# Seven-product matrix multiplication with K split into 256 + 256 + 64 or into 288 + 288: the last rows in one matmul per product

## The chip, the cores and the metric

One core of one Trainium2 chip. The metric is the device time of one execution, in microseconds (us); three executions of the kernel before were timed, and one more was profiled.

## The reference

x is 2048 x 576. It is normalised row by row, and three things are summed: x itself, a sliding attention (32 heads of 18, a window of 8 keys at distances 0, 2, ..., 14), and a dense block with ReLU.

```python
xn = (x - mean) / sqrt(var + 1e-5)
q, k, v = split(xn @ wqkv)                 # 576 x 1728, 32 heads of 18
o = softmax(q . k[s - 2w] * 18**-0.5) @ v[s - 2w]      # w = 0..7, masked before the start
h = maximum(xn @ w1, 0)                    # 576 x 4608
return x + o @ wo + h @ w2                 # wo 576 x 576, w2 4608 x 576
```

All inputs and the output are float32.

## The kernel before, in words

**Precision.** TensorE multiplies in a shortened float32 form (fp32r). Each operand is cut into a high part (ScalarE copies it, which rounds) and a low part (VectorE subtracts: `hi_lo`), and a product is the sum of three terms: high by high, high by low, low by high.

**Two halves of x.** x is worked through in two halves (`ph` 0 and 1) of 1024 rows; a half lies transposed in SBUF, in `h` = 0, 1 and `j` = 0, 1, groups of 256 columns. The first products are `xn @ w1` (18 sets of 256 features per half, kind F) and `xn @ wqkv` (7 sets, kind Q): 25 sets per half, 50 in all, each with two steps `t` (one per `h`).

**Seven products for eight.** From t = 4 on (sets 2 to 49) a step takes K = 576 as 256 + 256 + 64. The first 512 rows and the 256 features of a set are a 2 by 2 block matrix, multiplied by Strassen's scheme in Winograd's form: seven products P1 to P7 (`pstep`) of sums of weight blocks (made by VectorE in `set_make`: c1 to c4) by sums of x blocks (`s_forms`). Each is six matmuls (three terms by two groups of 128 rows; `terms`). The last 64 rows, `RR`, are not in the scheme: four of the products (P5, P2, P3, P4) take two more matmuls for them (`rest`), with x's high and low parts stacked in 128 rows (`XR`). Sets 0 and 1 are multiplied without the scheme (`classic`, 14 matmuls per product) in the opening.

**Results.** F results go through ReLU and a high/low split into one of six buffers `HB` (`h_parts`), and output steps `o_step` multiply them by `w2` into PSUM (`po`), six matmuls each. Q results are turned and stored in DRAM (`qd`), and attention is done by VectorE from there: `fetch` loads K, V and Q of one of four units, `attention` forms products with the window, softmax and the weighted sum; its output is turned through DRAM and multiplied by `wo` along with later output steps.

**Weights.** `w1`, `wqkv` and `w2` are copied in the first half to packed DRAM buffers (`w1c`, `wqc`, `w2c`) by DMAs on POOL's queue (`kept_part`, paced by a small POOL copy that follows ScalarE's `hb`). `set_make(s)` is called one set ahead, in step t = 2s - 2: four loads of 128 KB and two of 64 KB (the last 64 rows twice, for high and low), then the sums, then high and low parts into `wset`, of which there are two.

**Order.** The program is written out by a planner, `Order`. PE's order is fixed by the loops and, up to t = 4, by the list `OPEN`: B and O are output steps, T turns a tile of x, Q and F are products of sets 1 and 0, K copies a set to its packed buffers, S makes sums of x, M makes set 2. ScalarE's and VectorE's operations are put between by estimated durations, when their inputs are ready, by due times. Attention waits in a list `back`, which VectorE takes from when nothing else is ready soon. SP issues most DMAs in the planner's order, and an issue waits there for what it depends on; each engine works strictly in the order written.

**The second half of x** is loaded, normalised and turned during t = 47 to 51 (`x_load`, `x_norm`, `x_raw`, `x_rest`, `x_parts`, `x_done`), after the last attention unit of the first half.

Of the kernel before, what the change touches and what calls it, by code (L numbers as in the profile page):

```python
# [16 lines left out]
P = 128  # L17
NPH = 2
NI = 8
# [10 lines left out]
NHB = 6  # L30
# [10 lines left out]
T1, B11, T2, B21, T3, B22, T4, RR = range(8)  # L41
B12 = T3

PE, ACT, DVE, SP, PL = "pe", "act", "dve", "sp", "pool"
TAIL = {PE: 0.24, ACT: 0.13, DVE: 0.13}
# [3 lines left out]
class Op:  # L49


    __slots__ = ("eng", "dur", "fn", "after", "due", "end", "lag", "then", "post", "gate")

    def __init__(self, eng, dur, fn, after, due, lag=0.0):
        self.eng, self.dur, self.fn, self.due, self.lag = eng, dur, fn, due, lag
        self.after = [a for a in after if a is not None]
        self.end = None
        self.then = None
        self.post = None
        self.gate = None  # L60


class Order:
# [4 lines left out]
    def __init__(self):  # L68
        self.clk = {PE: 0.0, ACT: 0.0, DVE: 0.0, SP: 0.0, PL: 0.0}
        self.dma = 0.0  # L70
        self.gp = 0.0
        self.wait = {ACT: [], DVE: []}
        self.back = deque()
# [14 lines left out]
    def give(self, op, start):  # L88
        op.fn()
        self.clk[op.eng] = start + op.dur  # L90
        op.end = start + op.dur + TAIL[op.eng] + op.lag
        if op.then:
            op.then.end = self.gp = max(self.gp, op.end) + op.then.dur
        if op.post:
            op.post()

    def pick(self, eng):
        now = self.clk[eng]
        best, soon = None, None
        for op in self.wait[eng]:  # L100
            r = self.ready(op)
            if r is None:
                continue
# [7 lines left out]
        if eng == DVE and self.back:  # L111
            op = self.back[0]
            r = self.ready(op)
            if r is not None:
                s = max(now, r)
                if soon is None or s + op.dur <= soon[1] + self.SLACK:
                    return op, s
        return soon

    def step(self, limit):  # L120
        best = None
        for eng in (ACT, DVE):
            c = self.pick(eng)
            if c and c[1] < limit and (best is None or c[1] < best[1]):
                best = c
# [9 lines left out]

    def hurry(self, op, due):
# [5 lines left out]
    def force(self, ops):  # L142
        for op in ops:
            if op is None:
                continue
            self.hurry(op, -1.0)
            while op.end is None:
                if op in self.back:
                    assert self.step(FAR)
                else:  # L150
                    assert self.step(FAR), "an operation waits for what is not given out"
# [10 lines left out]

    def later(self, fn, n, after=(), lag=0.0):
# [4 lines left out]
    def send(self, fn, kb, after=(), margin=0.0):  # L168

        after = [a for a in after if a is not None]  # L170
        self.force(after)
# [9 lines left out]
    def keep(self, fn, kb, after=0.0):  # L181

        fn()
        op = Op(PL, 1.0, None, (), 0.0)
        self.clk[PL] = max(self.clk[PL], self.now(), after) + kb / 90.0
        op.end = self.clk[PL] + 3.0
# [21 lines left out]
def tile_body(ctx: ExitStack, tc: tile.TileContext, x, wqkv, wo, w1, w2, out):  # L208
# [6 lines left out]
    DR = D - KT * P  # L215
    D2 = D // 2
# [54 lines left out]
    mvp = pool("mvp", 6)  # L271
# [5 lines left out]
    act, dve, send, pe = o_.act, o_.dve, o_.send, o_.pe  # L277

# [9 lines left out]
    XR = [keep.tile([P, 3, TBN], F32R, name=f"xr{h}") for h in range(2)]  # L288
    keep.tile([P, PADS[0]], F32, name="pad0")
    BUF = [keep.tile([P, 2, 2048], F32R, name=f"wset{b}") for b in range(2)]  # L290
    keep.tile([P, PADS[3]], F32, name="pad4")
    HB = [keep.tile([P, 2, TBN], F32R, name=f"hb{b}") for b in range(NHB)]
    WHB = [keep.tile([P, 2, TBN], F32R, name=f"oh{b}") for b in range(2)]
    keep.tile([P, PADS[3]], F32, name="pad5")
# [15 lines left out]
    def wset(s):  # L310
        return BUF[s % 2].rearrange("p e (s k c) -> p e s k c", s=8, k=2)
# [27 lines left out]

    def mm(o, l, r, start, stop):  # L340
        nc.tensor.matmul(o, l, r, start=start, stop=stop, skip_group_check=True)  # L341

    def hi_lo(hi, lo, raw, n, after, slack, behind=(), by_pool=False):

        if by_pool:
            def both():
                copy(hi, raw)
                nc.gpsimd.tensor_tensor(lo, raw, f32(hi), op=ALU.subtract)

            a = act(both, n, after, slack)  # L350
            a.then = b = Op(PL, 0.0055 * n, None, (), 0.0)
            return [a, b]
# [9 lines left out]
    TURNED = [0] * NI  # L362
# [6 lines left out]
    def normalise(i, src, after, slack, by_act=False, alloc=True):  # L369
# [8 lines left out]
        def rest():  # L378
            z["mv"] = mv = mvp.tile([P, 2], F32, name="mv")
            z["r"] = r = mvp.tile([P, 1], F32, name="rstd")  # L380
# [3 lines left out]
            if by_act:  # L384
                z["nm"] = nm = mvp.tile([P, 1], F32, name="nm")
# [14 lines left out]

        if by_act:
            MEANS[i] = b
            NORMED[i] = act(one, D + 200, [b], slack + 1.0)
        else:
            NORMED[i] = dve(two, D // 2 + 100, [b], slack + 1.0)

    def turn_pe(i, pa, pb, after=()):
        def f():
            if pa is not None:
                for k in range(KT):  # L410
                    nc.tensor.transpose(pa[:, k * P : (k + 1) * P], XN[i][:, TURNED[i] + k * P : TURNED[i] + (k + 1) * P], ident)
            if pb is not None:
                nc.tensor.transpose(pb[0:DR, 0:P], XN[i][:, KT * P : D], ident)

        return pe(f, 0.11 * ((KT if pa is not None else 0) + (pb is not None)), [NORMED[i], *after])
# [7 lines left out]
    def xt_direct(i, pa, pb, t, slack, free):  # L423
# [7 lines left out]
        r1 = act(lambda: copy(XR[h][0:DR, j, c], pb[0:DR, 0:P]), 128, [t], slack + 1)  # L431
        r2 = dve(lambda: sub(XR[h][DR:P, j, c], pb[0:DR, 0:P], f32(XR[h][0:DR, j, c])), 128, [r1], slack + 1.5)
        if j == 0:
            r3 = act(lambda: copy(RD[h][0:DR, c], pb[0:DR, 0:P]), 128, [t, *free], slack + 4)
        else:
            r3 = dve(lambda: sub(RD[h][0:DR, c], RD[h][0:DR, c], pb[0:DR, 0:P]), 128, [t, *RAWR[h]], slack + 2)
        XOK.setdefault((h, j), []).extend([k1, k2, r1, r2])
        XHL.append((k1, k2))
        RAW.setdefault((h, j), []).append(k3)
        RAWR.setdefault(h, []).append(r3)  # L440
        return [k1, k2, k3, r1, r2, r3]
# [3 lines left out]
    def s_forms(h, slack):  # L445
# [15 lines left out]
        r = act(lambda: copy(XR[h][0:DR, 2], RD[h][0:DR]), TBN, RAWR[h], slack + 3)  # L461
        ok.append([r, dve(lambda: sub(XR[h][DR:P, 2], RD[h][0:DR], f32(XR[h][0:DR, 2])), TBN, [r], slack + 3.5)])
        XOK[h, 10 + S1], XOK[h, 10 + S2], XOK[h, 10 + S4] = ok
        return [z for y in ok for z in y]

# [46 lines left out]

    def set_make(s, fine=False):
# [6 lines left out]
        w = wset(s)  # L520
        z = f32(w)[:, 1]
        got = {}
        free = slots_free(s % 2, range(8))

        def rest_rows():
            for rows in slice(0, DR), slice(DR, P):
                got[RR] = send(
                    lambda rows=rows: nc.sync.dma_start(z[rows, RR, :, 0:wd], src_[KT * P : D, :].rearrange("r (k c) -> r k c", k=2)),
                    64, [*there, *free], late,
                )  # L530

        for rows, f, b in ((0, 0, B11), (0, 1, B12), (256, 1, B22), (256, 0, B21)):
            ts = b == B12
# [1042 lines left out]
```

## Time and profile before

| | |
|---|---|
| median of three runs | 1112.38 us (1112.16 to 1112.78) |
| the profiled execution, its own time | 1115.05 us |
| its span, first to last instruction | 1113.3 us |
| granted TensorE clock | 0.999 |
| PE busy | 1102.5 us, 9047 matmuls |
| VectorE (DVE) busy | 909.0 us, 1749 instructions |
| ScalarE (ACT) busy | 756.2 us, 1561 instructions |
| GpSimd (POOL) busy | 218.3 us, 434 instructions |
| DMA | 144.15 MB, mean 129 GB/s |

A row of a timeline has start, duration, engine, line, operation, output and inputs, partitions x elements, count, and in brackets the idle time of the engine before it with what ended it. A grouped row has, behind the bar, the busy sum in us, the mean of one in ns, and the idle time before the group by releaser. PEld is the weight load, which runs beside the matmuls; SPq is the queue of SP. Matmul ends are modelled, starts are not. A row of DMA issues has count, KB each and the median us from issue to landing.

### The profile page before, as it was taken

What the parts mean: (1) busy time and instruction counts of PE and PEld (TensorE: products, weight loads), DVE (VectorE), ACT (ScalarE), POOL (GpSimd) and SP (SyncE); (2) the same over time, 40 slices, a digit from 0 to 9 for tenths busy, and PEclk for the clock granted to TensorE, in tenths of its full rate; (3) what the DMA queues carried; (4) which work ended last, traced back from release to release, by engine and by line L of the source; (5) the groups of instructions that cost most, each with busy time, mean ns of one, the idle gap of its engine ahead of it and who ended that gap; (6) DMA issues with size and microseconds to landing.
All of it is one profiled execution on the core that took longest, in us unless ns stands there. A gap on an engine that the chain in (4) does not pass through costs nothing.

```text
span 1113.3 us, 24046 instructions
## 1 busy us (share of the span) xinstructions
PE 1102.5 (99%) x9047; PEld 1098.6 (99%) x9047; DVE 909.0 (82%) x1749; ACT 756.2 (68%) x1561; POOL 218.3 (20%) x434
## 2 busy tenths in 40 slices
PE   9999999999999999999999999999999999999998
PEld 8998999999999999999999999999999999999998
DVE  7867999999999889955885689989998998997440
ACT  6754666566687677676794565656667766766774
POOL 4132384342554423700210000000000000000000
PEclk9999999999999999999999999999999999999999
DMA  7488488856854552463354745563625415224212
GB/s 218 105 187 199 122 216 192 184 145 169 213 158 127 163 151 84 107 158 92 110 173 93 192 93 110 122 137 83 158 76 117 107 52 141 70 56 86 78 49 86
DMA packets 329862, 144.15 MB, mean 129 GB/s; under 512 B 212097, under 2 KB 310401, under 8 KB 328513
## 3 DMA queue, kind: packets, MB, share of 16 engines
q1 hardware_dynamic: 320176, 115.76, 42.3%
q0 software_dynamic: 9408, 26.55, 8.3%
q8 instruction: 71, 1.16, 0.4%
q14 instruction: 47, 0.38, 0.1%
q10 hardware_dynamic: 160, 0.30, 0.1%
HBM read 118.42 MB, written 50.66 MB: 152 GB/s over the span
## 4 chain that ended last, share of the span: by engine, by line
PE 89%; DVE 3%; SPq 3%; DMA 2%; ACT 2%; issue 1%; POOL 0%; DVEq 0%; ACTq 0%
PE po L341 43%; PE bk L341 26%; PE pm L341 12%; PE bkA L341 7%; SPq L1061 1%; DMA qo<-qd 1%; DMA wset<-w1c 1%; DMA qo<-in_w 0%; DVE pr L1107 0%; DMA wqc<-in_wqkv 0%; DVE sn L338 0%; DVE stg L656 0%; DVE wset L338 0%; ACT x L335 0%; ACT hb L335 0%
## 5 line engine op out<-in xcount | busy, mean ns | idle before, releaser
L341 PE MATMUL po<-w2t,hb 128*128 128x256 f32 (+1 forms) x3456 | 503.5, 292 | 0.1
L341 PEld LDWEIGHTS po<-w2t,hb 128*128 128x128 f32 x3456 | 463.2, 187 | 0.4 <-DVE hb L628 0.4
L335 ACT ACTIVATE x<-po 128x576 f32<-128x576 f32 x286 | 186.3, 651 | 231.5 <-PE po L341 230.6
L341 PE MATMUL bk<-xs,wset 128*128 128x256 f32 (+1 forms) x1584 | 224.0, 277 | 0.6 <-ACT sn L335 0.6
L341 PEld LDWEIGHTS bk<-xs,wset 128*128 128x128 f32 (+1 forms) x1584 | 202.3, 187 | 0.9 <-ACT sn L335 0.8
L335 ACT ACTIVATE po<-x 128x576 f32<-128x576 f32 x286 | 187.0, 654 | 6.0
L481 POOL COPY spare<-hb 1x1 f32<-1x1 f32 x192 | 94.6, 493 | 222.8 <-ACT hb L335 222.8
L341 PE MATMUL bk<-xa,wset 128*128 128x256 f32 (+1 forms) x888 | 125.5, 278 | 1.8 <-DVE sn L338 0.9
L341 PEld LDWEIGHTS bk<-xa,wset 128*128 128x128 f32 (+1 forms) x888 | 113.7, 187 | 2.8 <-DVE sn L338 1.1
L341 PE MATMUL pm<-xs,wset 128*128 128x256 f32 (+1 forms) x720 | 102.2, 277 | 0.3 <-ACT bkA L335 0.3
L338 DVE TENSOR_TENSOR sn<-bk,sn 128x256 f32<-128x256 f32 (+1 forms) x132 | 55.2, 419 | 52.3 <-ACT hb L335 25.3
L341 PEld LDWEIGHTS pm<-xs,wset 128*128 128x128 f32 (+1 forms) x720 | 92.0, 187 | 0.7 <-ACT bkA L335 0.5
L1107 DVE TENSOR_TENSOR pr<-qo,kk 128x1152 f32<-128x1152 f32 x64 | 85.4, 1346 | 7.9 <-DMA qo<-qd 6.9
L1113 POOL TENSOR_SCALAR_AFFINE_SELECT lg<-lg 1x512 f32<-1x512 f32 x8 | 9.6, 1206 | 415.1 <-DVE lg L1110 415.1
L341 PE MATMUL bkA<-xa,wset 128*128 128x256 f32 (+1 forms) x624 | 88.3, 278 | 0.5 <-ACT bkA L335 0.5
L1110 DVE TENSOR_REDUCE lg<-pr 128x64 f32<-128x1152 f32 x64 | 85.3, 1340 | 0.2
L1139 DVE TENSOR_TENSOR pr<-lg,v 128x1152 f32<-128x1152 f32 x64 | 85.2, 1348 | 0.2
L341 PEld LDWEIGHTS bkA<-xa,wset 128*128 128x128 f32 (+1 forms) x624 | 81.4, 187 | 1.0 <-ACT bkA L335 0.7
L335 ACT ACTIVATE hb<-sn 128x256 fp32r<-128x256 f32 x140 | 57.4, 414 | 35.1 <-DVE sn L338 34.6
L341 PE MATMUL bk<-xr,wset 128*128 128x256 f32 (+1 forms) x412 | 80.4, 276 | 0.0
L338 DVE TENSOR_TENSOR wset<-ts,wset 128x512 fp32r<-128x512 f32 (+2 forms) x98 | 65.1, 665 | 10.5 <-ACT wset L335 10.3
L1146 DVE TENSOR_TENSOR pr<-pr 128x288 f32<-128x288 f32 (+1 forms) x128 | 71.4, 597 | 0.0
(156 smaller groups left out, 1551.8 us busy)
## 6 DMA issues: line engine op xcount, KB each, us to landing
w2t<-w2c SPq DMA_DIRECT2D x70, 288.0 KB, 3.3
qd<-stg SPq DMA_DIRECT2D x216, 64.0 KB, 2.0
wset<-w1c SPq DMA_DIRECT2D x105, 128.0 KB, 2.8
w1c<-in_w POOLq DMA_DIRECT2D x68, 144.0 KB, 3.4
w2c<-in_w POOLq DMA_DIRECT2D x68, 144.0 KB, 3.5
out<-x SPq DMA_DIRECT2D x16, 288.0 KB, 2.2
ts<-w1c SPq DMA_DIRECT2D x35, 128.0 KB, 2.7
wset<-w1c SPq DMA_DIRECT2D x70, 64.0 KB, 2.3
```

What stands on the lines that cost most here:

```text
L335: nc.scalar.activation(o, i, func)
L338: nc.vector.tensor_tensor(o, a, b, op=op)
L341: nc.tensor.matmul(o, l, r, start=start, stop=stop, skip_group_check=True)
L481: nc.gpsimd.tensor_copy(spare[0:1], f32(LATEST[-1])[0:1, 0:1])
L1061: z = send(lambda: nc.sync.dma_start(o, i.rearrange("i p c -> p i c")), cnt * 2, after)
L1107: nc.vector.tensor_tensor(pr[i], q, window(k, i), op=ALU.mult)
L1110: nc.vector.tensor_reduce(s["lg"][:, i], pr.pop(i).rearrange(heads, d=Dh), axis=AX.X, op=ALU.add)
L1113: nc.gpsimd.affine_select(out=z, in_=z, pattern=[[1, NI], [1, W], [0, HG]], compare_op=ALU.is_ge, fill=-1e9 / scale, base=1 - W, channel_m ...
L1139: nc.vector.tensor_tensor(pr[i].rearrange(heads, d=Dh), e, window(VV[u % 2], i).rearrange(heads, d=Dh), op=ALU.mult)
L1146: nc.vector.tensor_tensor(o, z[:, 0:n], z[:, n : 2 * n], op=ALU.add)
```

## The change

K is split into two halves of 288 rows, each 256 + 32 (`ROWS = (0, 288)`). The 32 rows of each half go through the seven-product scheme too. Their three terms lie in one matmul of 128 rows: the weight side holds low, high, high, zero, the x side four copies of the 32 rows of which the first two are high and the last two low. So each product is `terms` and one `rest` matmul:

```diff
+        def go(o, b, xs, xr, start, more):
+            def f():
+                terms(o, slot(m, b), xs, start)
+                rest(o, m, b, xr)
+            return pe(f, T7, [*ok[b], *more])
...
-    def rest(bank, s, f, xr):
-        w, wd = wset(s), wide(s)
-        for e in range(2):
-            mm(bank[0:wd], w[:, e, RR, f, 0:wd], xr, False, e == 1)
+    def rest(o, s, b, xr, stop=False):
+        wd = wide(s)
+        mm(o[0:wd], wset(s)[0][:, b, 2, 0:wd], xr, False, stop)
```

The weights' sums and parts for these rows are made once for four sets at a time, in 128 rows (32 of each set), and kept in DRAM as low, high, high. There are seven batches for the 25 sets; `KK`, the buffer of attention's keys, is the work space. Batches 0 and 1 stand in `OPEN` as W0 and W1; 2 and 3 follow the first attention unit's key products, 4 and 5 the second's, 6 the fourth's, and the next unit's keys are fetched after them.

```diff
+    def batch(b, work, highs, free, slack):
...
+        def there(got):
+            c1 = dve(lambda: sub(raw[0:n, 0:3:2], raw[0:n, 2:5:2], raw[0:n, 1:3]), 2 * P, got, slack)
+            c2 = dve(lambda: sub(raw[0:n, T2], raw[0:n, B22], raw[0:n, T1]), P, [c1], slack + 0.2)
+            c4 = dve(lambda: sub(raw[0:n, T4], raw[0:n, B21], raw[0:n, T2]), P, [c2], slack + 0.4)
...
+                e = [send(lambda: nc.sync.dma_start(RWD[b][0], work[0:n, 0 : 7 * P]), 115 * n // DH, ds)]
...
+                        e.append(send(lambda: nc.sync.dma_start(to[:, y], c), 58 * n // DH, ks))
```

`set_make` loads a set's remainder ready made, in one DMA of 96 rows, in place of the two of 64 rows, and every product of the set waits for it. One part of 512 columns becomes one of 256, because `RR` is gone.

```diff
-                    lambda rows=rows: nc.sync.dma_start(z[rows, RR, :, 0:wd], src_[KT * P : D, :].rearrange("r (k c) -> r k c", k=2)),
-                    64, [*there, *free], late,
+        last = send(
+            lambda: nc.sync.dma_start(
+                f32(hi)[0:R3, :, 2], RWD[b][:, i * DH : (i + 1) * DH].rearrange("a r (s c) -> a r s c", s=7)
+            ), 344, [BDONE[b], *free], late,
+        )
+        ok = {q: [last] for q in range(7)}
```

For sets 0 and 1 in the opening the 32 rows are loaded three times over by a source with a leading repeat:

```diff
+    def thrice(src, r0):
+        return src[r0 : r0 + DH][None].to_broadcast([3, DH, src.shape[1]])
```

The x side: POOL makes the four copies (`fours`, in the tile of the attention's logits), and two transposes per tile turn them; four sums and two pairs of parts per half `h` follow (`s_forms`, `s_rest`, the latter in the place of an `XA` block that only `classic` reads).

```diff
+        def fours():
+            src = XN[i].rearrange("p (q c) -> p q c", q=2)[:, :, 2 * P : 2 * P + DH]
+            nc.gpsimd.tensor_copy(XF[0][:, i % 2], src[:, :, None, :].to_broadcast([P, 2, 4, DH]))
...
+            for q in range(2):
+                z = XF[0][:, i % 2, q].rearrange("p a c -> p (a c)")
+                nc.tensor.transpose(pb[:, q * P : (q + 1) * P], z, ident)
```

To make room in SBUF the hidden buffers fall from six to four. The list `OPEN` is new, in another order, with R (turn a remainder of x) and W (a batch) as added kinds:

```diff
-NHB = 6
+NHB = 4
-B0 T2 B1 T3 Q000 K2 F010 F011 T4 Q011 O0101 T5 O0100 S0 O0110 T6
-Q001 K3 O0111 Q010 T7 F100 F101 F110 O1000 S1 O1001 O1010 F111 M2 K4 O1011
-Q111 Q100 Q110 O1100 O1101 O1111 Q101 O1110
+K2 T2 B0 T3 R2 W0 B1 K3 R3 T4 R4 Q001 F011 S0 T5 Q010 F010 Q000 Q011 T6 R5
+R6 K4 O0100 O0101 O0110 T7 R7 O0111 F100 F111 F101 W1 F110 S1 M2 O1000 Q111
+O1010 O1001 O1011 Q101 Q110 O1101 O1100 O1111 O1110 Q100
```

Further: the planner now also places POOL's operations, and when something is forced it gives out only what that needs; eight transposes of the attention output by VectorE become one instruction; the second half's tiles are loaded in one DMA each instead of two, from t = 47 on in other places; the last group of the first half's attention output is planned one step later.

More of the change, by code (lines that the diff above doesn't have):

```diff
@@ L134, in step, with needs @@
         return True
+    def needs(self, op, out):
+        if op.end is None and op not in out:
+            out.add(op)
+            for a in op.after:
+                self.needs(a, out)
+        return out
     def hurry(self, op, due):
@@ L161, in dve, with gp @@
         return op
+    def gp(self, fn, n, after, slack):
+        op = Op(GP_, 0.0022 * n + 0.2, fn, after, self.now() + slack)
+        self.wait[GP_].append(op)
+        return op
     def later(self, fn, n, after=(), lag=0.0):
@@ L345, in hi_lo @@
         if by_pool:
[L346 to L352, printed above, removed]
+            a = act(lambda: copy(hi, raw), n, after, slack)
+            return [a, o_.gp(lambda: less(lo, raw, f32(hi)), n, [a], slack + 0.8)]
         a = act(lambda: copy(hi, raw), n, after, slack)
```

618 lines of the change are left out of this document (391 added, 227 removed).

## The prediction

> **What bounds the kernel now.** I read the page's busy times and slices first, then busy time by stage, the waits of PE, and the PE timeline. The page:
>
> ```profile
> span 1113.3 us, 24046 instructions
> PE 1102.5 (99%) x9047; PEld 1098.6 (99%) x9047; DVE 909.0 (82%) x1749; ACT 756.2 (68%) x1561; POOL 218.3 (20%) x434
> PE   9999999999999999999999999999999999999998
> PE 89%; DVE 3%; SPq 3%; DMA 2%; ACT 2%; issue 1%; POOL 0%; DVEq 0%; ACTq 0%
> ```
>
> PE is idle for 1113.3 - 1102.5 = 10.8 us in all, and the chain that ended last is PE for 89%. So a matmul taken out should take its time out of the span, unless a new wait is put in its place. Where waits can arise shows by stage (columns: busy us and count of PE, PEld, DVE, ACT, POOL, then clock, DMA share, GB/s):
>
> ```profile
> 0.00:20.00 20.00, 17.56 (x124) 16.38 (x125) 12.95 (x38) 13.76 (x32) 9.53 (x20) 1.00 0.87 242
> 20.00:60.00 40.00, 39.46 (x329) 38.62 (x328) 32.16 (x76) 27.45 (x61) 7.15 (x18) 1.00 0.48 119
> 60.00:105.00 45.00, 42.61 (x350) 41.95 (x350) 30.85 (x64) 24.63 (x53) 14.70 (x42) 1.00 0.86 207
> 105.00:300.00 195.00, 195.00 (x1621) 195.00 (x1621) 183.73 (x341) 126.79 (x263) 88.73 (x202) 1.00 0.71 175
> 300.00:500.00 200.00, 200.00 (x1638) 200.00 (x1637) 172.62 (x317) 147.69 (x300) 83.29 (x133) 1.00 0.51 138
> 500.00:660.00 160.00, 158.70 (x1309) 158.05 (x1308) 113.22 (x237) 108.67 (x228) 10.11 (x16) 1.00 0.52 130
> 1050.00:1113.30 63.30, 59.28 (x478) 59.05 (x476) 19.17 (x42) 38.14 (x75) 0.00 (x0) 0.99 0.21 68
> ```
>
> From 105 to 500 us PE never waits; its idle time is 2.4 us in 0 to 20, 2.4 in 60 to 105, 1.3 in 500 to 660 and 4.0 at the end, where the last stores drain. Three places can go wrong: the opening (to 60 us, DVE 80% busy from 20 on), 60 to 105 us, where DMA is at 0.86, and the change to the second half of x (500 to 660).
>
> **The change, part by part.**
>
> *Fewer matmuls.* Before, each of the 96 steps (t = 4 to 99, two per weight set) runs seven products of six matmuls, and the last 64 rows of K cost two more in four of them (P5, P2, P3, P4): 42 + 8 = 50. After, every half of K is 256 + 32 rows, and the 32 rows' three terms (low by high, high by high, high by low) fill one matmul of 128 rows: 7 x 7 = 49. The 16 products of the opening keep 14 each. What a matmul costs is read from starts, since the ends are modelled:
>
> ```profile
> 303.35 0.85 PE L341 MATMUL bk<-xs,wset 128*128 128x256 f32 x6
> 304.04 0.39 PE L341 MATMUL bk<-xr,wset 128*128 128x256 f32 x2
> 304.26 1.72 PE L341 MATMUL po<-w2t,hb 128*128 128x256 f32 x12
> ```
>
> Eight matmuls from 303.35 to 304.26, so 0.114 us each, the remainder's no cheaper than the others. 96 x 0.114 = **-10.9 us**.
>
> *More transposes.* The remainder of x is now turned two times per tile (two groups of 32 columns, each four times over, made by a POOL copy). In the opening 8 single ones become 16; in the second half of x four become 16: +20.
>
> ```profile
> 27.14 0.60 PE L411 MATMUL bk<-ident,pr 128*128 128x128 f32 x4
> 27.57 0.27 PE L413 MATMUL pm<-ident,pr 128*64 128x128 f32 x1
> ```
>
> Four in 0.43 us, 0.11 each: 20 x 0.11 = **+2.2 us**. So PE's own work is 8.7 us less.
>
> *The opening (DVE, ACT, POOL, SP).* Durations:
>
> ```profile
> L338 DVE TENSOR_TENSOR wset<-wset 128x512 fp32r<-128x512 f32 x90 | 60.5, 684 | 2.3 <-ACT wset L335 2.0
> L338 DVE TENSOR_TENSOR ts<-wset,ts 128x256 f32<-128x256 f32 x138 | 55.6, 412 | 6.1 <-DMA wset<-wqc 3.2 <-DMA wset<-w1c 2.3
> 18.17 0.28 DVE L338 TENSOR_TENSOR xr<-bkA,xr 64x128 fp32r<-64x128 f32 x1
> L335 ACT ACTIVATE wset<-wset 128x512 fp32r<-128x512 f32 x90 | 55.3, 620 | 0.0
> ```
>
> A batch (four sets' remainders in 128 rows) is a sum of 256 columns (0.41), two of 128 (0.28 each, the nearest row) and a low part of 896 (684 + (684 - 412) x 384 / 256 = 1.09 us): 2.1 us of DVE and about 1.0 of ACT. In the opening DVE gains two batches (4.2), the sums of x's remainder (8 x 0.41 = 3.3), their low parts (4 x 0.68 = 2.7, less the old 2 x 0.41), wider low parts of x (8 x 0.14 = 1.1), and loses four subtractions of 0.28 and a weight part of 0.41: together +9.0. From 20 to 60 us it has 40 - 32.16 = 7.8 free; the second batch is first used by set 6 and can slip. ACT gains some 6.5 and has 12.5. On POOL:
>
> ```profile
> 8.50 2.21 POOL L348 TENSOR_TENSOR wset<-stg,wset 128x256 fp32r<-128x256 f32 x3 [0.70 <-ACT wset L335]
> 14.44 1.42 POOL L348 TENSOR_TENSOR w2t<-qo,w2t 128x576 fp32r<-128x576 f32 x1
> 7.83 0.58 DVE L399 TENSOR_SCALAR pr<-x,mv,rstd 128x576 f32<-128x576 f32 x1 [0.67 <-POOL rstd L383]
> 10.21 0.72 PE L341 MATMUL bk<-xa,wset 128*128 128x256 f32 x4 [0.43 <-ACT xa L335]
> 12.36 0.39 PE L341 MATMUL bk<-xr,wset 128*128 128x256 f32 x2
> ```
>
> The copy of tile 1's columns starts after 7.83 + 0.58 and takes some 0.74 (2.21 / 3, the nearest row); the remainders' transposes stand in PE's queue ahead of the first product and end near 10.1, against its start at 10.21: just hidden. Then POOL makes the low part of the first remainder (512 columns, about 1.4 as the 576) and two more of 0.74, done near 12.8, while the first last-row matmuls stand at 12.36. On SP the two batches add some 26 issues, in a gap that the queue has:
>
> ```profile
> 19.42 0.63 SPq L1260 DMA_DIRECT2D w2c<-in_w  x1
> 34.84 4.17 SPq L668 DMA_DIRECT2D qd<-stg  x8
> ```
>
> 15 us without an issue. For the opening I take **+1.5 us** (bounds 0, all hidden, and 5, where most of the 9.0 lies on the path), near the lower end because 7.8 of 9.0 has room.
>
> *60 to 105 us (DMA).* A set's remainder is now one load of 96 rows of 7 x 128 floats, 344 KB, against two of 64 KB, and every product waits for it. Three sets are loaded here: 3 x 0.213 MB more = 0.64 MB, 3.1 us at 207 GB/s, while 14% of 45 us, 6.3 us, are free. It lands two steps ahead of its use, and a step is (1113.3 - 60) / 96 = 11 us on average against 2.8 us for the nearest load below; set 3, whose load stands at 57.32 and whose first product at 66.34, has only 9. What a late landing costs here is seen in before:
>
> ```profile
> wset<-w1c SPq DMA_DIRECT2D x105, 128.0 KB, 2.8
> 57.32 0.45 SPq L537 DMA_DIRECT2D wset<-w1c  x1
> 66.34 0.94 PE L341 MATMUL bk<-xa,wset 128*128 128x256 f32 x6
> 89.66 1.36 DVE L1107 TENSOR_TENSOR pr<-qo,kk 128x1152 f32<-128x1152 f32 x1 [3.96 <-DMA qo<-qd]
> 93.12 0.97 PE L341 MATMUL pm<-xa,wset 128*128 128x256 f32 x6 [1.53 <-DVE sn L338]
> 95.18 0.97 PE L341 MATMUL bk<-xa,wset 128*128 128x256 f32 x6 [0.85 <-DVE sn L338]
> ```
>
> DVE stands in order at the first attention product for 3.96 us until the fetch lands; the sums that empty PSUM queue behind it, and PE loses 2.38. A microsecond later costs a microsecond. I take **+1.0** (bounds -2.4, this wait gone, and +8, below), near the lower end because the bytes fit.
>
> *Second half of x.* Twelve of the transposes are already counted. DVE gains the four sums (1.6) and two low parts (1.4) per half and loses about as much as one part of 512 and one sum, +1.6 each, 3.2 in all, with 47 us free from 500 to 660. PE lost 1.3 there. **+0.5** (0 to 2).
>
> *At nothing.* Five later batches: 10.5 us of DVE between 105 and 500, with 38.6 free, less 0.27 per set that the smaller low part saves; if that room were gone, attention would end later and its output be late for the steps that add it. Batches after an attention unit occupy K's buffer while DVE still works on that unit's V. The hidden buffers fall from six to four: of a step's four new pieces the first two find buffers freed by the output steps ahead of them, the third waits for the output step behind P3 and the fourth for the last one ahead of P4; nobody needs the third before the next step's first output, about 3 us on. Without that cover each would cost an eviction, 0.4 us of ACT and as much of DVE. The 8 x 8 transposes of attention output that become one instruction save DVE overhead only.
>
> **Sum.** 1113.3 - 10.9 + 2.2 + 1.5 + 1.0 + 0.5 = 1107.6 us of span, 5.7 less. The profiled execution took 1115.05 with its 1113.3 of span, 2.67 above the runs' median of 1112.38; the same difference from the median gives 1106.7.
>
> **Rivals.**
>
> (a) *The remainder loads are slow, and the gain is eaten between 60 and 105 us.* Seen from DRAM the load's outermost extent is three (low, high, high). If the chip deals a transfer out by that, three of 16 engines move it. At full share 16 engines would move 207 / 0.86 = 241 GB/s, 15 each, so 344 KB take 7.6 us; three of them ask 23 us of engines with 6.3 left, 16.6 too much; of that perhaps 9 us are cache copies of POOL's queue, which can slip. Some 8 us stay, on set 3 above all, with its 9 us. 1112.4 - 8.7 + 1.5 + 0.5 + 8 = 1113.7 (1110 to 1116). For it: nothing else in this stage has slack. Against: a rate per engine on one transfer is shown by no row.
>
> The Trainium skill, page "DMA: Bandwidth & Descriptors", section "Rules for kernel authors", says that an outermost dimension below 16 confines the whole DMA to at most that many engines, and gives a leading broadcast as the example. By that rule this rival's time holds; no transfer of the trace of before has so short an outermost extent, so nothing here confirms or denies it.
>
> (b) *Slower: the first attention fetch.* K's buffer is also the work space of batch 1, so the fetch waits until that batch has been stored (1.4 MB, 6.7 us at 207 GB/s, after loads, sums and parts), then competes with the larger loads. PE's loss at 91 us must grow by 9.4 us over the 1105.7 that is left without it (1112.4 - 8.7 + 1.5 + 0.5) to come out above the band of no change; at 12 later it gives 1117.7. For it: the 3.96 us that are already there. Against: in the trace K's fetch begins only at 75.91,
>
> ```profile
> kk<-in_wqkv SPq DMA_DIRECT2D x4, 128.0 KB, 4.5
> 40.14 0.38 SPq L537 DMA_DIRECT2D wset<-wqc  x1
> 75.91 6.42 SPq L1061 DMA_DIRECT2D kk<-qd  x5
> ```
>
> and batch 1 stands ahead of set 2's loads (40.14 in before): with loads as the nearest (4.5), 3.1 of sums and parts and 6.7 of store it is done near 55.
>
> (c) *The stalls go as well.* The order of the opening is new; with the 2.4 us at 91 to 95 gone and the opening's 1.5 hidden, 1112.4 - 8.7 - 2.4 + 0.5 = 1101.8 to 1104. For it: nothing else stands in PE's way.
>
> That the matmuls might not fall in number isn't open: it is written out.
>
> **How the numbers follow.** Forecast 0.52 (1103.5 to 1109.5), (a) 0.22, (b) 0.10, (c) 0.16. Within 0.2%, 1110.2 to 1114.6, is about what a measurement of this kernel can't tell from no change. Faster: 0.52 + 0.16 + 0.06 of (a) = 0.74; the same: 0.12, from (a) and a little of (b); slower: 0.14, (b) and the top of (a). The range from 1102 to 1114 leaves out most of (b), the top of (a) and the lowest of (c).
>
> **What would show it.** Remainder matmuls 704 instead of 800 and 8971 matmuls in all; starts still 0.114 apart; PE busy near 1094; idle before PE of some 12 to 14 us. (a) shows as PE or DVE waits on a remainder load and landings above 7 us, (b) as a wait on K's or Q's fetch. Wrong I am if PE waits between 105 and 500, or if the opening loses more than 5 us.

## The result, and the profile after

The changed kernel takes 1167.8 us (median of 4 runs, 1166.1 to 1171.2) against 1112.6 for the kernel before on the same chip: ratio 1.0488, interval [1.0449, 1.0528]. That is 55 us slower, where 5.7 us faster was forecast. The head of its page (busy time, PE's busy tenths and granted clock in 40 slices, the chain that ended last):

```profile
span 1165.7 us, 23990 instructions
PE 1109.6 (95%) x8971; PEld 1101.4 (94%) x8971; DVE 915.3 (79%) x1721; ACT 757.9 (65%) x1573; POOL 215.0 (18%) x453
PE   7987986898989999999999989999999999999998
PEclk9999998899989999999999999999999999999999
PE 81%; DMA 8%; SPq 5%; DVE 3%; ACT 2%; issue 1%; DVEq 0%; ACTq 0%
```

PE issues 8971 matmuls, 76 fewer than before, as forecast. It is idle for 1165.7 - 1109.6 = 56.1 us instead of 10.8, and its busy time is 1109.6 instead of the 1093.8 that fewer matmuls should have left: behind long waits the clock falls (0.95 to 0.97 in five of the stages below). The chain has DMA and SP's queue for 13% instead of 5%. By stage (columns as in the prediction):

```profile
0.00:20.00 20.00, 13.78 (x99) 12.63 (x99) 10.37 (x29) 12.44 (x28) 10.85 (x24) 1.00 0.73 219
20.00:60.00 40.00, 37.34 (x306) 36.32 (x307) 34.86 (x80) 29.15 (x60) 11.57 (x26) 1.00 0.61 165
60.00:105.00 45.00, 37.54 (x294) 36.43 (x293) 23.27 (x57) 22.54 (x51) 14.53 (x42) 0.96 0.80 197
105.00:200.00 95.00, 83.06 (x665) 82.09 (x664) 70.71 (x128) 50.52 (x104) 32.57 (x85) 0.95 0.67 168
200.00:300.00 100.00, 88.51 (x706) 87.86 (x705) 83.62 (x156) 55.60 (x119) 34.88 (x78) 0.95 0.75 189
300.00:400.00 100.00, 94.04 (x743) 93.39 (x742) 82.40 (x141) 66.66 (x136) 41.36 (x89) 0.97 0.67 193
400.00:500.00 100.00, 100.00 (x819) 100.00 (x819) 90.26 (x152) 72.75 (x151) 39.19 (x66) 1.00 0.53 148
600.00:700.00 100.00, 94.18 (x759) 92.32 (x758) 69.03 (x146) 64.97 (x138) 6.34 (x12) 0.97 0.58 146
```

A full stage has 819 matmuls in 100 us, 0.122 us each on average over all widths; with this a stage's missing matmuls become time. From 105 to 400, where PE never waited before, the three stages hold 665 + 706 + 743, instead of 795 + 828 + 820. The waits (who waits and on which line, who ended the wait; us in all, times, longest):

```profile
PE po L386 <- ACT po L377: 10.4, 3, 10.0
PE pm L386 <- DVE sn L380: 7.6, 2, 7.4
PE bk L386 <- DMA wset<-rwd: 7.4, 4, 4.0
PE pm L386 <- DMA wset<-rwd: 4.1, 1, 4.1
DVE kk L380 <- DMA kk<-in_w: 15.5, 3, 8.2
DVE kk L380 <- DMA kk<-in_wqkv: 14.2, 3, 11.4
ACT kk L377 <- DMA qo<-qd: 11.2, 1, 11.2
```

Five waits, 11.5 us, are on the remainder load (`wset<-rwd`) itself. The two longest, 10.0 on ACT and 7.4 on DVE, go back to batch loads (`kk<-in_w`, `kk<-in_wqkv`) that are late: DVE and ACT work in order and stand at a batch's first sum and its high part, and PE behind them. (For ACT's wait the profile names a Q fetch, `qo<-qd`, issued behind the batch's loads; ACT stands at the part made of the batch's sums.) The lines behind one another, from the timelines of SP, DVE and PE (start, duration; idle time before it and its releaser in brackets):

```profile
55.15 0.78 SPq L711 DMA_DIRECT2D wset<-rwd  x1
56.47 6.55 SPq L838 DMA_DIRECT2D qd<-stg  x4
63.81 0.38 PE L386 MATMUL bk<-xr,wset 128*128 128x256 f32 x1 [2.27 <-DMA wset<-rwd]
...
162.70 6.23 SPq L683 DMA_DIRECT2D kk<-in_w  x2
...
188.16 0.77 SPq L711 DMA_DIRECT2D wset<-rwd  x1
188.97 9.44 SPq L683 DMA_DIRECT2D kk<-in_w  x2
203.42 0.43 DVE L380 TENSOR_TENSOR kk<-kk 128x256 f32<-128x256 f32 x1 [8.22 <-DMA kk<-in_w]
208.44 0.79 PE L386 MATMUL pm<-xa,wset 128*128 128x256 f32 x2 [7.42 <-DVE sn L380]
```

A remainder load issued at 55.15 lets PE go at 63.81, 8.7 us later. And what SP issues next stands: two batch loads take 9.44 us to issue behind the remainder load of 188.16. The one issue right behind a remainder load takes over 2 us behind 36 of the 48, 4.1 in the median. How many engines move the load shows once the transfers ahead of it are done (stages of 1 us, after):

```profile
58.00:59.00 1.00, 1.00 (x10) 1.00 (x9) 0.46 (x1) 0.81 (x2) 0.00 (x0) 1.00 0.19 57
```

A DMA share of 0.19 (0.22 in each of the next two) is three of 16 engines. So two accounts are possible. **Theory A**: the one-DMA remainder load, whose source is three blocks, runs on three engines, lands late and holds up SP's queue. **Theory B**: the later batches and the extra transfers cost by themselves, however they are dealt out. Smaller rivals were the opening's order and the four hidden buffers.

### The profile page after: what moved, and what is told of

The parts are those of the page before. It is cut to its first block, busy times and chain, and to the rows that moved or that the text cites. A ratio compares the mean times of both kernels' runs of the same rounds, so it can differ in the third digit from the quotient of the medians.

```text
span 1165.7 us, 23990 instructions
## 1 busy us (share of the span) xinstructions
PE 1109.6 (95%) x8971; PEld 1101.4 (94%) x8971; DVE 915.3 (79%) x1721; ACT 757.9 (65%) x1573; POOL 215.0 (18%) x453
## 4 chain that ended last, share of the span: by engine, by line
PE 81%; DMA 8%; SPq 5%; DVE 3%; ACT 2%; issue 1%; DVEq 0%; ACTq 0%
PE po L386 38%; PE bk L386 24%; PE pm L386 12%; PE bkA L386 6%; DMA wset<-rwd 3%; DMA kk<-in_w 3%; SPq L683 2%; SPq L1232 1%; SPq L707 1%; DMA stg<-in_w 1%; ACT x L377 0%; DVE xa L380 0%; DMA oh<-turned 0%; DVE kk L380 0%; DVE wset L380 0%
## 5 line engine op out<-in xcount | busy, mean ns | idle before, releaser
L386 PE MATMUL po<-w2t,hb 128*128 128x256 f32 (+1 forms) x3456 | 508.5, 294 | 16.1 <-ACT po L377 10.4
L386 PEld LDWEIGHTS bk<-xs,wset 128*128 128x128 f32 (+1 forms) x1584 | 205.6, 189 | 2.6 <-ACT bkA L377 2.1
L386 PE MATMUL bk<-xa,wset 128*128 128x256 f32 (+1 forms) x1152 | 199.0, 280 | 7.6 <-DVE sn L380 5.0
L386 PEld LDWEIGHTS bk<-xa,wset 128*128 128x128 f32 (+1 forms) x1152 | 165.0, 189 | 9.0 <-DVE sn L380 5.8
L569 POOL COPY spare<-hb 1x1 f32<-1x1 f32 x192 | 85.3, 444 | 270.0 <-ACT hb L377 269.9
L386 PE MATMUL pm<-xa,wset 128*128 128x256 f32 (+1 forms) x540 | 94.2, 282 | 7.8 <-DVE sn L380 7.6
L386 PEld LDWEIGHTS pm<-xa,wset 128*128 128x128 f32 (+1 forms) x540 | 77.6, 190 | 8.7 <-DVE sn L380 8.3
```

The source lines that it names most:

```text
L569: nc.gpsimd.tensor_copy(spare[0:1], f32(LATEST[-1])[0:1, 0:1])
```

## The experiments

Ratios are against the kernel before, timed on the same chip.

**The remainder load as three DMAs of 32 rows**, all else as after:

```diff
-            lambda: nc.sync.dma_start(f32(hi)[0:R3, :, 2], RWD[b][:, i * DH : (i + 1) * DH]...),
+            lambda: [nc.sync.dma_start(f32(hi)[a * DH : (a + 1) * DH, :, 2], RWD[b][a, i * DH : (i + 1) * DH]...) for a in range(3)],
```

> The changed kernel; only the load of a set's remainder (96 rows of 7 x 128 floats) is issued as three DMAs of 32 rows each instead of one whose source has an outermost extent of three; the planner's order is unchanged. Theory 1 (three of 16 DMA engines carry the load, 8.5 us instead of 3, and SP's next issue waits behind it): most of the 55 us goes, 1106 to 1120 us, the waits of PE on the remainder load vanish, SP's issues behind it take under 1 us each, and the clock is back at 0.99 or more. Theory 2 (DVE stands in order at the batches' own loads, whatever the remainder load does): 1145 us or more. Theory 3 (four hidden buffers and the new opening order): 1140 or more.

1126.8 us, ratio 1.0111 [1.0096, 1.0127]: 41 of the 55 us are this one transfer, the same bytes with two issues more per set (theory 1 had expected 1120 at most). SP's timeline of this kernel:

```profile
54.34 2.51 SPq L711 DMA_DIRECT2D wset<-rwd  x3
56.94 2.17 SPq L838 DMA_DIRECT2D qd<-stg  x4
156.57 1.20 SPq L683 DMA_DIRECT2D kk<-in_w  x2
```

The same four `qd` stores that took 6.55 us to issue take 2.17, and the same two batch loads 1.20 instead of 6.23. Behind none of the 48 remainder loads does the next issue take over 1.6 us. No wait on `rwd` is left. In the spans, 39.7 us shorter, 30.9 are idle time of PE and 8.8 its busy time. But 13 to 14 us stay, though PE has 8.7 us less to do.

**The other loads with a short outermost extent spread too** (the opening's triple loads, the batches' `w1` loads), with the remainder load spread and with it left as it is:

```diff
-    send(lambda: nc.sync.dma_start(ST1[0:R3, 4 + v, y], thrice(wq_s[:, y, 0:P], ROWS[v] + 2 * P)), 48)
+    send(lambda: [nc.sync.dma_start(ST1[a * DH : (a + 1) * DH, 4 + v, y], wq_s[ROWS[v] + 2 * P : ...]) for a in range(3)], 48)
```

> As the kernel with three DMAs per remainder load, and also the opening's triple loads as three DMAs each and the batches' loads of two or three sets of w1 as one DMA per set. Theory 1: 1102 to 1112 us, a few us under the kernel with only the remainder load spread, the rest of it in the first 20 us. Theory 2, in the form that the batches' loads are slow by themselves because of their own outermost extent of two: the larger part of the 55 us goes only here. Theory 3: 1135 or more.

> The changed kernel with the opening's triple loads and the batches' loads spread, but the remainder load left as it was. Theory 1: 1155 to 1165 us, some 5 us less in the opening. Theory 2: under 1130. Theory 3: no change, 1162 to 1170.

1128.4 (1.0133 [1.0098, 1.0168]) and 1171.3 us (1.0512 [1.0491, 1.0533]). These loads, few and not repeated per set, are no part of the loss: spreading them brings nothing. In the first of the two the opening's first product starts at 10.9 instead of 12.6, but a later transpose then waits 3.0 us, and PE's idle time up to 105 us stays at 11.7.

**The converse: transfers added to the kernel before.** 48 DRAM copies that nothing waits for, one per set made.

```diff
+        send(lambda: nc.sync.dma_start(MORE[s][:, :, 0:P], SRC), 295, [*there, *free], late)
```

`SRC` stands for rows of `w1`: in the first run 576 of them as three blocks of 192, in the second the same 576 plainly, in the third three blocks of 160 with gaps between them (and the destination to match).

> The kernel before, with one more DMA per set on SP, ahead of the set's sums: 295 KB from w1 to an unused DRAM buffer, source in three blocks of 192 rows, 512 bytes per row. Nobody reads it. Theory 1: 20 to 50 us slower than before, with SP's next issue behind it at 5 us or more. Theories 2 and 3: within 5 us of before, since DMA's mean share rises by under 0.02.

> The kernel before with the same 295 KB more per set on SP as in the run with three blocks (which took 13 us more than before), but the source is counted in 576 rows, so that all 16 engines share it. Theory 1 (it is the three engines, not the bytes): within 4 us of before. Theory B (the bytes and the additional issue are what costs): 9 to 14 us slower, like the other.

> The kernel before with 48 more transfers from DRAM to DRAM, of 246 KB each, put where the sets are made, whose source is three blocks of 160 rows with a gap of 32 rows between them, so that the blocks can't be taken together; nothing waits for them. It leaves nothing out of the computation. Theory A (a transfer in three blocks runs on three engines, and SP can't issue behind it): SP's next issue stands 4 to 9 us behind each, other loads that share these engines land late, and the time is 1140 to 1165. Rival (the shape costs nothing by itself, only a consumer that waits for it): within 4 us of the 1128 that the same number on all engines gave.

1126.4 (1.0109 [1.0089, 1.0129]), 1128.0 (1.0117 [1.0084, 1.0150]) and 1141.5 (1.0237 [1.0203, 1.0272]). The first was no test: its three blocks of 192 rows lie evenly spaced, so they are one run of 576 rows (its instruction carries 576 rows in the trace, as the plain one does), and it took what the plain source took, with the same median from issue to landing (4.4 and 4.3 us). So 48 well-dealt transfers of 288 KB cost 12 to 13 us (theory B has a part), and in three true blocks, though a sixth smaller, 13 more. SP's next issue takes over 2 us behind 29 of these 48, 5.1 at most, and behind none of the others. The key product of attention, whose operands are fetched through SP's queue, shows where (the group in the run with all engines, then with three blocks; last column idle time before it):

```profile
L1113 DVE TENSOR_TENSOR pr<-qo,kk 128x1152 f32<-128x1152 f32 x64 | 85.5, 1346 | 3.1 <-DMA qo<-qd 3.0
```

```profile
L1113 DVE TENSOR_TENSOR pr<-qo,kk 128x1152 f32<-128x1152 f32 x64 | 85.1, 1345 | 20.0 <-DMA qo<-qd 17.0 <-DMA turned<-pr 2.8
```

Nobody waits for the added transfers; other loads come late because of them. Whether they are late by SP's standing issue or by the three busy engines, no run separates.

**Four hidden buffers alone, in the kernel before** (`NHB = 6` to `4`):

> The kernel before with four buffers of the hidden units instead of six, alone. Prediction (the buffers cost nothing, since PE is the bound and the planner keeps them short-lived): 1111 to 1114, no new wait of PE on hb. Rival (part of the loss is from the smaller buffers): 1116 or above with PE waiting for DVE hb.

1116.4 us, ratio 1.0018 [1.0009, 1.0028]: 2 us (1 to 3) in the times, above the 1114 that was expected at most, while its profile has a span of 1113.2, as before, and PE waits for `hb` once, for 0.2 us. So this edit costs 3 us at most, and the profile does not show where.

**Later sums of the batches.** In the kernel with three DMAs the largest wait left starts at batch 2: DVE and ACT stand at its sums, and PE 4.8 us at 168.79. (The rows name a Q fetch as the releaser; the wait of DVE that ends last, at 164.9, is on the batch's own last load, issued at 161.2.)

```profile
165.19 0.43 DVE L380 TENSOR_TENSOR kk<-kk 128x256 f32<-128x256 f32 x1 [6.15 <-DMA qo<-qd]
166.73 0.95 ACT L377 ACTIVATE kk<-kk 128x896 fp32r<-128x896 f32 x1 [6.00 <-DMA qo<-qd]
168.79 3.25 PE L386 MATMUL po<-w2t,hb 128*128 128x256 f32 x12 [4.80 <-ACT po L377]
```

The planner was told that batch loads land 8 us later, so that it puts their sums later: for batches 2 to 6 (2 us for the first two), for batch 2 alone, and for 2 to 5.

```diff
-    got.append(send(lambda: nc.sync.dma_start(dst, src), kb, free))
+    got.append(send(lambda: nc.sync.dma_start(dst, src), kb, free, 8.0 if b > 1 else 2.0))
```

> The kernel with three DMAs per remainder load, and the planner told that the batches' own loads land 8 us later than it reckons (2 us for the two in the opening), so that VectorE's and ScalarE's first operations on them are written further back. Theory 4 (what is left between 105 and 200 us, 6.6 us of idle PE and the slow clock behind it, is DVE and ACT standing in order at batches 2 and 3): 8 to 12 us less than the 1126.8 of that kernel, 1115 to 1119, PE idle under 2 us from 105 to 300. Theory 5 (the batches' work itself, DVE and DMA, is too much there): within 3 us of 1126.8.

> The kernel with the remainder loads as three DMAs, with 8 us of margin on the loads of batch 2 alone. Theory 7 (what is left of the loss after the loads are spread is one place: the planner puts batch 2's sums on DVE and ACT before their loads and stores have landed, at 158 to 168 us, and DVE and ACT stand in order): the 4.80 us wait of PE at 168 goes, 105 to 200 us has near 790 matmuls instead of 707, and the time is 1115 to 1119 instead of 1127, since the end of attention isn't moved by the later batches. Rival (the time is only moved on, as with the margin on all batches): 1125 or above, with new waits of PE between 500 and 540.

> As the one before, with the margin of 8 us on the loads of batches 2 to 5, not on the last one, which follows unit 3 of the attention. If it is the last batch's margin that pushed the end of attention together in the run with all batches: 1113 to 1119, no wait of PE over 5 us between 500 and 540. If it is the middle batches' margin: 1135 to 1145, with the two waits of 11.7 and 5.4 us at 516 and 523 there again.

1143.5 (1.0263 [1.0241, 1.0285]), 1125.8 (1.0107 [1.0092, 1.0122]) and 1144.4 (1.0289 [1.0253, 1.0325]). The margin for all makes 105 to 200 us full, and loses more elsewhere (timeline of SP and PE of that run):

```profile
234.12 1.66 SPq L1232 DMA_DIRECT2D kk<-qd  x3
349.81 3.53 SPq L1232 DMA_DIRECT2D kk<-qd  x6
516.11 1.65 PE L386 MATMUL bk<-xa,wset 128*128 128x256 f32 x6 [11.74 <-DVE sn L380]
523.40 1.65 PE L386 MATMUL bk<-xa,wset 128*128 128x256 f32 x6 [5.43 <-DVE sn L380]
```

The keys of units 1 and 2 are fetched only at 234 and 350 (203 and 308 without margin), attention ends at 522 instead of 515, and the planner then runs its last unit on DVE in one piece while PE waits. For batch 2 alone the 4.8 us go, and half of it is lost again behind 200 us (786 matmuls instead of 812): of the 8 to 12 us that were expected nothing clear is left (1125.8 against 1126.8). For batches 2 to 5 the waits at 516 and 524 are there again, with 12.1 and 5.6 us, so it is the middle batches' margin that makes them.

**The opening's order and another layout in scratch**, both on top of the margin: first the raw order with the remainders last, then `RWD` kept per set as 96 rows, so that one DMA has 96 as its outermost extent.

```diff
-RAWS = ((C11, 0, 0), (C21, 1, 0), (None, 0, 0), (C12, 0, 1), (C22, 1, 1))
+RAWS = ((C11, 0, 0), (C21, 1, 0), (C12, 0, 1), (C22, 1, 1), (None, 0, 0))
-    RWD = [dram.tile([3, len(z) * DH, 7 * P], F32, ...)]
+    RWD = [dram.tile([len(z), R3, 7 * P], F32, ...)]
```

> As the kernel with the margin, and in the opening the remainders of sets 0 and 1 (the triple loads, still on three engines) are loaded behind the four main blocks instead of between them. Theory 6 (the triple load delays the blocks behind it, which PE's first product waits for at 12.4 instead of 10.2 us): 2 to 5 us less than the kernel with the margin alone, and the first product starts before 11 us. Otherwise: the same within 2 us, the opening's loss is DVE and ACT work.

> As the kernel with margin and order of loads, but the batches' results are kept in DRAM set by set, 96 rows each, so that a remainder load is again one DMA, with 96 as its outermost extent; a batch is stored by three DMAs per set instead of three in all. Theory 1: the load runs on all engines as with three DMAs, so 0 to 4 us less than that kernel (96 SP issues fewer for the loads, 54 more for the stores), and SP's issue behind a remainder load takes under 1 us. If the length of the load and not its outermost extent were the cause, it would be back at 1150 or more.

1146.5 (1.0281 [1.0258, 1.0305]) and 1151.1 (1.0320 [1.0298, 1.0342]). The order moves the first product back to 13.4, not forward; the layout has none of the loss at `rwd`, neither waits of PE on it nor a standing issue behind it (2.0 us at most), so 336 KB in one DMA is not what costs. It was still 5 us slower than the run with the order, where 0 to 4 faster was expected: its first product starts at 15.0, and the margin's waits stand at 528 and 535 with 14.4 and 5.7 us. That its additional stores do this is not shown.

**The later batches left out**, and only their sums left out:

```diff
     def batch_now(b, free, then=()):
+        if b > 1:
+            o_.force(free); BDONE[b].end = o_.now()
+            ...
+            return
```

```diff
+            if b > 1:
+                ds = ks = got          # the second run: stores follow the loads, no sums and parts
```

Both leave out part of the computation.

> The kernel with the remainder loads as three DMAs, without batches 2 to 6: their loads, sums, parts and stores are left out, K is fetched without waiting for them, and the sets that need them load the rows of batch 1 (so the products of those sets' remainders are wrong). Batches 0 and 1 of the opening stay. Theory (the later batches, costed at nothing in the prediction, are what is left of the loss behind 105 us): 105 to 600 us full, the opening loss of about 6 us stays, time 1108 to 1114. Rival (what is left lies elsewhere: the remainder loads themselves, the stores, the opening): 1120 or above.

> As the kernel with three DMAs, but batches 2 to 6 have no sums and parts: their loads and stores and the place of the K fetch behind them stay, DVE and ACT do nothing for them (so the stored rows are unprocessed weights). Theory a (the loss is DVE and ACT standing in order at a batch's sums until loads land): like the run without the later batches, 1108 to 1116. Theory b (the loss is the K fetch, 55 to 60 us later in units 1 and 2, and the transfers on SP's queue): within 4 us of 1127.

1115.1 (1.0007 [0.9991, 1.0022]) and 1129.0 (1.0128 [1.0107, 1.0149]). So batches 2 to 6 cost some 12 us, and taking away their sums and parts alone wins nothing. Page and stages without the batches, and the stage from 105 to 200 in the run with them (the first experiment):

```profile
PE 1094.3 (98%) x8971; PEld 1089.4 (98%) x8971; DVE 906.3 (81%) x1701; ACT 752.8 (68%) x1568; POOL 214.7 (19%) x453
```

```profile
0.00:20.00 20.00, 13.62 (x99) 12.75 (x99) 10.22 (x28) 12.21 (x28) 11.30 (x24) 1.00 0.71 213
20.00:60.00 40.00, 36.19 (x286) 35.08 (x286) 34.44 (x79) 29.45 (x60) 11.90 (x26) 0.96 0.62 168
60.00:105.00 45.00, 42.57 (x354) 41.94 (x352) 28.24 (x69) 24.54 (x56) 14.75 (x42) 1.00 0.92 240
105.00:200.00 95.00, 94.63 (x792) 94.63 (x793) 88.09 (x162) 61.55 (x131) 46.26 (x107) 1.00 0.73 182
```

```profile
105.00:200.00 95.00, 88.42 (x707) 87.79 (x706) 79.49 (x145) 54.81 (x114) 34.77 (x90) 0.95 0.71 183
```

85 matmuls, 10.4 us, are lost between 105 and 200, where batches 2 and 3 stand. Without the sums, the rows put the loss on SP's queue (timelines of that run, and one of its stages of 5 us):

```profile
169.58 2.58 SPq L689 DMA_DIRECT2D kk<-in_w  x2
179.58 0.34 SPq L672 DMA_DIRECT2D rwd<-kk  x1
181.17 0.90 SPq L713 DMA_DIRECT2D wset<-w1c  x1
184.89 0.42 ACT L377 ACTIVATE wset<-wset 128x256 fp32r<-128x256 f32 x1 [8.46 <-DMA wset<-w1c]
185.34 0.43 DVE L380 TENSOR_TENSOR ts<-ts,wset 128x256 f32<-128x256 f32 x1 [8.16 <-DMA ts<-w1c]
186.16 1.65 PE L386 MATMUL pm<-xa,wset 128*128 128x256 f32 x6 [6.46 <-DVE sn L380]
```

```profile
185.00:190.00 5.00, 3.85 (x17) 3.69 (x18) 4.66 (x12) 3.82 (x8) 0.00 (x0) 0.50 0.81 175
```

SP stands from 172.2 to 179.6 at batch 3's store, which may not be issued before the batch's loads have landed; the next set's loads stand behind it and come at 181.2, against 161.1 in the run without the batches. With the sums in, DVE and ACT stand at batch 2 instead, as the rows at 165 to 169 above show.

**Batch 5 moved to another unit; K made late without batches.** With the batches the keys of later units are fetched later, for unit 1 at 203 us instead of 158 without them (148 in the kernel before), for unit 2 at 308 instead of 267. Is that the cost?

```diff
-    BAFTER = {0: (2, 3), 1: (4, 5), 3: (6,)}
+    BAFTER = {0: (2, 3), 1: (4,), 2: (5,), 3: (6,)}
```

```diff
+            def late(t=KFREE[0][0], z=z):      # in the run without batches, u < 2
+                t.end = z.end + 45.0
```

> As the kernel with three DMAs, with batch 5 made after unit 2 of the attention instead of behind batch 4 after unit 1, so that K of unit 2 is fetched one batch earlier. Theory b (the late K fetch costs): 1119 to 1124, K's fetch for unit 2 near 290 instead of 308 us. Theory a: within 3 us of 1127.

> The kernel without batches 2 to 6 (their loads, sums, parts and stores are left out, the sets load batch 1's rows), with K of units 1 and 2 fetched 45 us after the buffer is free, as it comes with the batches. Theory b: 1124 to 1130. Theory c: 1113 to 1118, as without the delay.

1127.7 (1.0119 [1.0102, 1.0136]) and 1116.8 (1.0015 [1.0002, 1.0028]). Batch 5 moved brings K of unit 2 at 296 instead of 308, and no gain. With K at 189 and 313 us and no batches the time is that without the delay, within 2 us. The late fetch is not the cost, up to these times; unit 1's own 203 was not reached.

**The batches on another queue**: their loads and stores issued by GpSimd, and then with the margin for batches 2 and 3 as well.

```diff
-    nc.sync.dma_start(dst, src)
+    (nc.gpsimd if b > 1 else nc.sync).dma_start(dst, src)
```

> The kernel with three DMAs, with the loads and stores of batches 2 to 6 issued by GpSimd instead of SyncE; K is still fetched behind the batches and nothing is left out. Theory c (what costs is SP's order: the store of batch 3, issued behind loads that have not landed, holds up the next set's loads by 20 us): no wait of PE over 3 us between 160 and 200, time 1113 to 1119. Theory b (the late K fetch): within 4 us of 1127. Against theory c stands one risk: GpSimd's own copies of the weights come behind the batch's waits, and then PE waits for sets that are not copied yet.

> The kernel with three DMAs, with the loads and stores of batches 2 to 6 issued by GpSimd, and 8 us of margin on the loads of batches 2 and 3, so that the planner puts their sums later. Nothing is left out. Theory (two orders share the 12 us: SP's, where the batch's stores stand ahead of the next set's loads, and DVE's and ACT's, where the sums stand until the batch's loads land; taking one away leaves the other): 105 to 200 us has 785 or more matmuls and the time is 1114 to 1119. Rival (the transfers' bytes themselves make the sets' loads late, whichever queue issues them): 1123 to 1128, with PE waiting behind set loads between 105 and 300.

1128.4 (1.0116 [1.0090, 1.0142]) and 1147.2 (1.0292 [1.0275, 1.0310]); both expectations of a gain failed. With the batches on GpSimd's queue SP issues the set's first load in time (158.9), but DVE stands at batch 2's sum and PE behind it, as on SP (the row names a transfer of the same queue as the releaser):

```profile
162.47 0.42 DVE L380 TENSOR_TENSOR kk<-kk 128x256 f32<-128x256 f32 x1 [4.31 <-DMA w2c<-in_w]
166.07 3.15 PE L386 MATMUL po<-w2t,hb 128*128 128x256 f32 x12 [2.95 <-ACT po L377]
```

With the margin too, a third queue shows:

```profile
170.99 0.38 ACT L377 ACTIVATE hb<-bk 128x256 fp32r<-128x256 f32 x1 [4.81 <-POOL spare L569]
171.71 1.65 PE L386 MATMUL bk<-xs,wset 128*128 128x256 f32 x6 [5.01 <-ACT bkA L377]
```

GpSimd paces its weight copies by a small copy that reads a hidden buffer (`spare`, L569); it now comes later, behind the batch's issues, so ACT can't write that buffer and waits 4.8 us. And K comes at 238 and 326, past what was free: attention ends at 526, with PE waits of 8.0 and 5.5 us at 520 and 527.

## Why the prediction was wrong

*Matmuls and transposes* (-10.9 and +2.2, so 1093.8 of PE): right. In the run without the later batches PE is busy for 1094.3, with 8971 matmuls. After has the same matmuls and 15.3 us more, with a clock of 0.95 to 0.97 in five stages where the other run has 1.00.

*The remainder load*, the step that failed. The sum has it as +1.0, from 60 to 105 us, because its bytes fit there. Its mechanism stood in rival (a), at chance 0.22 and 8 us (for the 9 us of copies that "can slip" there, it gives no row); it measured 41. Three errors made it small. It was priced from 60 to 105 us alone, as if later stages had room because PE never waited there. Between after and the first experiment the missing matmuls are 42 in 60 to 105, 42 in 105 to 200, 106, 68 and, from 600 to 700, 78: 336 x 0.122 = 41 us, near the 39.7 of the spans. It was priced by the engines' free time, as if others' packets made room; that SP stands behind such a load, up to 8.7 us for one issue, was not in it. And a late microsecond was priced as one microsecond, when a longer wait has half the clock behind it. The Trainium skill, page "DMA: Bandwidth & Descriptors", section "Rules for kernel authors", has the rule that a leading extent below 16 limits the engines of a DMA. By that rule the chance should have been nearer to one: the change's source has extent three, and the trace after agrees, with a DMA share of 0.19, three of 16 engines, while the load runs.

*Five later batches at nothing*: some 12 us. The prediction counted DVE's free time (38.6 us for 10.5), and taking the sums away alone indeed won nothing. It did not name who is queued behind the batch on SP, DVE and ACT: a store that waits for loads, and sums that wait for them. It named the late end of attention as the risk; that came only at K fetches of 232 us or later, in runs with margin, which took 17 to 19 us longer than the same kernels without it.

*The opening and 60 to 105 us* (+1.5 and +1.0): PE's idle time up to 105 is 6.4 + 3.8 + 2.4 = 12.6 us without the later batches, against 5.4 before, so 7.2 instead of 2.5, and all of it before 60, where the bound was 5. After, the first product starts at 12.6 instead of 10.2 and waits for the copies of `xa`; the prediction had left it in its place, with the remainders' transposes just hidden ahead of it. Spreading the loads brought it to 10.9 without bringing the time back, turning the order moved it to 13.4; the cause of the opening's loss stays open.

*Hidden buffers* at nothing: right within 3 us. *Rival (b)*, K's fetch: no; *(c)*: the stalls stayed.

The account in the profiled spans: -8.2 (PE's work, 1102.5 to 1094.3) + 7.2 (opening) + 1.7 (other idle) + 12.0 (later batches) + 39.7 (remainder loads) = 52.4, from 1113.3 to 1165.7. It comes out because each term is a difference between runs one edit apart, and shows nothing further. The prediction's own conditions for being wrong, waits between 105 and 500 and an opening that loses more than 5 us, both came true. No kernel of these beat the one before: with the loads spread and the later batches left out it is level, at 1115.1, since the opening gives back what the matmuls save. Whether SP's order and DVE's and ACT's order are all of the batches' 12 us is not shown, as the run that was to show it met a third queue.

## What to carry to other kernels

Look at the outermost extent of every added DMA before its bytes: 336 KB in three blocks cost some 41 us over 48 loads, and three DMAs of one block each took that away with two more issues. An engine with a fifth or a third of its time free (DVE and ACT here) still works in order: for each added wait ask on every queue (SP's, GpSimd's, DVE's, ACT's) who stands behind it, and price that. Moving the waiting transfers to another queue changed here who stood, not whether.

## What was not expected of the hardware

A queue stands behind a badly dealt transfer: two issues that took 1.2 to 1.3 us took 6.2 and 9.4 behind a load in three blocks, and the trace has this as the issue's own duration, not as a wait for something. Equally spaced blocks that touch counted as one run: three of 192 rows landed in 4.4 us, 576 in 4.3. After a PE wait of 6.5 us the clock was 0.50 for the next 5 us, and 17 matmuls took 3.85 us, 0.23 each instead of 0.114. The Trainium skill, page "TensorE: Matmul & The Clock Gate", section "Part 1: The HAM clock gate (the "warmup" mystery)", gives half clock behind an idle window of about 3.4 us, which agrees. So a long wait cost more than its length here.
